# Windowed attention and two feed-forwards: the plan takes VectorE's and GpSimd's SBUF-only instructions to exclude each other, and its order is searched anew

## The chip, the core and the metric

One core of a Trainium2 chip runs one program. Its engines work side by side, each through its own queue in order: TensorE (PE; PEld is its loading of weights), VectorE (DVE), ScalarE (ACT), GpSimd (POOL) and SyncE (SP), which issues most transfers. The metric is the device time of one execution in microseconds (us), as the median of several.

## What is computed

The reference, cut to what matters. The attention keeps four sink columns and a window of 128 keys; its output, 1536 rows of 512, goes through two feed-forwards with 2048 hidden columns.

```python
# batch 2, heads 8, seq 768, head_dim 64; n_sink 4, window 128
scores = scale * np.matmul(q, k.transpose(0, 1, 3, 2))
keep = is_sink | in_window                 # 0 <= row - column < window
scores = np.where(keep, scores, -1e9)
a = softmax(scores)
x = matmul(a, v)                           # as 1536 x 512
h = x @ w_in                               # first feed-forward, 2048 hidden
g = np.where(h >= 1, h, np.where(h <= -1, 0.0, (h + 1) ** 2 / 4))
x = g @ w_out
h = x @ w2_in                              # second feed-forward
r = np.maximum(h, 0.0)
return (r * r) @ w2_out
```

## The kernel before

The attention runs in 24 units (batch, block of 256 rows, pair of heads). In a unit, TensorE turns keys and queries (kind tp), VectorE copies them (tpc), TensorE makes scores for two halves (s), VectorE adds the mask and finds the row's minimum (m), ScalarE takes the exponential (e), VectorE the reciprocal of the sum (n), GpSimd scales the probabilities (pm) and copies the sink columns (sp), TensorE turns the probabilities (x, ts), ScalarE copies them (xc, tsc), TensorE multiplies with the values (av), and ScalarE and VectorE split the result into a high and a low part (xh, xl).

The feed-forwards are split into chunks of 128 hidden columns, 16 for each, in nine passes (PASSES): 3, 3, 4, 3 and 3 chunks for the first, four times 4 for the second. A step is one pass over a range of rows: first the hidden matmuls (L353), for which ScalarE (u; L360 or L362), VectorE (t, L367, which reads only SBUF, then g, L385; in the second feed-forward sq5, L369) and ScalarE and GpSimd (gc, L374, and gl, L378: the high and the low part of the result) work in turn; then the output matmuls (L421), whose sums VectorE adds up in SBUF (ad; L458, L460). The last pass of the first feed-forward also splits the sum for the second (yc, L437, and yl, L439). The twelve steps of passes 0 and 1 (STEPS) have 256 rows and lie between the attention's units; all later ones have 512.

The weights come as 64-bit numbers and are split into two parts by the kernel, each chunk in two halves (w_in, w_out), 64 halves in all: ScalarE takes two pieces of the raw words (ca, L275 and L279), VectorE works on them in four steps (c1 to c4; L292, L293, L285, L295), ScalarE makes the high part (cc, L296) and GpSimd the low one (cl, L297). All halves share one temporary buffer (wt=1), and nine chunks fit into the ring of split weights (six until the attention ends).

The order of all engines is made before the program is written, by a planner in Python. Each step is a Task with an engine, a time for which it holds the engine and one until its result is there (COST: engine, step, took, extra), the tasks it waits for and the buffers it takes. Planner.run always takes the task that can start first; among equals the one with the least key goes first. KEYS, STEPS, SPREAD, LOADS, PARTS and LEAD set the keys; LEAD says by how much the loads and the splits of a late pass's weights rank ahead of the pass itself, whose three steps have keys three apart. The program then issues every engine's instructions in the planned order, and semaphores carry the dependencies. In gaps of TensorE in the attention, warm_gaps puts filler matmuls (L855).

In the planner before, a VectorE task with a last figure over 0 in COST (c1, c2: 0.58; c3: 0.15; c4: 0.2; t: 0.4; t5: 0.3) is lengthened by that share of its overlap with GpSimd tasks. GpSimd tasks are never lengthened:

```python
if t.engine == "DVE" and t.extra:
    more = sum(max(0.0, min(b, at + took) - max(a, at)) for a, b in gps[-3:]) * t.extra
    step, took = step + more, took + more
```

Of the kernel before, what the change touches and what calls it, by code (L numbers as in the profile page):

```python
# [43 lines left out]
    q=2, v=VB, k=KB, p=PB, pt=PTB, sm=4, sp=2, st=2, vs=1, av=2, sc=SCB, tp=TPB, tx=TXB, f=PSF,  # L44
# [1 line left out]
)  # L46
LATE = dict(f=8 - PSF, w=RING - EARLY, G=G1, U=2, T=2)
KEYS = dict(
    q=-56.88, v=92.12, kd=-49.39, kp=-74.72, tp=29.38, tpc=-1.63, kp0=-102.23, s0=0.45,
    m0=-45.61, e0=40.66, s1=0.52, m1=-63.12, e1=101.70, n=2.30, pm0=81.97, sp0=34.55,  # L50
    pm1=-18.03, sp1=39.22, x0=-80.79, xc0=-63.27, x1=8.31, xc1=-25.32, ts=-67.22, tsc=91.12,
    tsl=-29.67, av=38.69, xh=78.19, xl=-127.41,
)
STEPS = [
    (0, 0, 112.72), (0, 256, -26.70), (0, 512, -74.02), (1, 0, -2.04), (1, 256, -58.87),
    (1, 512, 70.12), (0, 1024, -23.65), (0, 768, 33.74), (1, 1024, -32.96), (1, 768, 82.54),
    (0, 1280, -2.66), (1, 1280, 10.87),
]
SPREAD = 8.10, 8.20
LOADS = [24.08, -24.48, 25.55, -33.69, -88.64, 43.67]  # L60
PARTS = [13.07, 11.19, -49.96, 70.04, -43.43, 138.90]
START = 8700.0
LEAD = 125.99, 87.06
LAG = dict(PE=53, ACT=33, DVE=33, POOL=78, SP=40)
COST = dict(
    q=("SP", 2200, 0, 2320), v=("SP", 1100, 0, 1160), kd=("SP", 500, 0, 230), wi=("SP", 500, 0, 1470),
    wo=("SP", 500, 0, 1270), vs=("SP", 900, 0, 200), od=("SP", 500, 0, 800),
    kp=("POOL", 139, 189, 0), kp0=("POOL", 139, 189, 0), vsm=("POOL", 200, 240, 0),
    pm=("POOL", 1012, 1060, 0), pms=("POOL", 562, 615, 0), sp=("POOL", 139, 203, 0),
    cl=("POOL", 1235, 1275, 0), gl=("POOL", 690, 740, 0), gl5=("POOL", 1240, 1290, 0),  # L70
    yl=("POOL", 690, 740, 0), yl5=("POOL", 1240, 1290, 0),
    tp=("PE", 436, 600, 0), s=("PE", 640, 709, 0), ss=("PE", 415, 492, 0), x=("PE", 436, 600, 0),
    xx=("PE", 327, 490, 0), ts=("PE", 218, 380, 0), av=("PE", 1230, 1390, 0), avv=("PE", 790, 870, 0),
    mm=("PE", 120, 283, 0), mm5=("PE", 226.7, 390, 0),
    e=("ACT", 994, 1100, 0), es=("ACT", 780, 880, 0), xc=("ACT", 492, 587, 0), xxc=("ACT", 375, 478, 0),
    tsc=("ACT", 270, 367, 0), xh=("ACT", 270, 370, 0), ca=("ACT", 575, 672, 0), cc=("ACT", 525, 620, 0),
    u=("ACT", 365, 465, 0), gc=("ACT", 310, 405, 0), u5=("ACT", 585, 680, 0), r5=("ACT", 500, 590, 0),
    gc5=("ACT", 525, 620, 0), yc=("ACT", 310, 405, 0), yc5=("ACT", 525, 620, 0), oda=("ACT", 450, 2500, 0),
    tpc=("DVE", 600, 686, 0), m=("DVE", 700, 780, 0), ms=("DVE", 430, 505, 0), n=("DVE", 375, 375, 0),
    tsl=("DVE", 335, 417, 0), xl=("DVE", 335, 417, 0), c1=("DVE", 425, 425, 0.58),  # L80
    c2=("DVE", 425, 425, 0.58), c3=("DVE", 687, 687, 0.15), c4=("DVE", 685, 685, 0.2),
    t=("DVE", 335, 418, 0.4), g=("DVE", 335, 420, 0), ad=("DVE", 335, 417, 0),
    t5=("DVE", 600, 690, 0.3), g5=("DVE", 600, 690, 0), ad5=("DVE", 600, 687, 0),
    sq5=("DVE", 600, 690, 0), mask=("DVE", 1156, 1156, 0), vsc=("DVE", 1600, 1600, 0),
)
TURNS = "tp", "x", "xx", "ts"
CUTS = ((0, 3, 6, 10, 13, 16), (0, 4, 8, 12, 16))
PASSES = [
# [30 lines left out]
class Planner:  # L119
# [28 lines left out]
    def switch(self, last, t):  # L148
        if last is None or t.engine != "PE":
            return 0.0  # L150
        if t.kind in ("s", "ss"):
            return 90.0
        if last.kind in TURNS:
            return 50.0 if t.kind in TURNS else -80.0
        return 0.0

    def run(self):
        free = {pool: [(0.0, i) for i in range(n)] for pool, n in self.slots.items()}
        ready = {e: [] for e in LAG}
        idle = {e: self.begin for e in LAG}  # L160
        dma, gps, pe = self.begin, [(0.0, 0.0)], None
        for t in self.tasks:
            t.wait, t.ready = len(t.after), self.begin
            if not t.wait:
                ready[t.engine].append(t)
        order = []
        while len(order) < len(self.tasks):
            best = None
            for e, tasks in ready.items():
                for t in tasks:  # L170
                    at = self.starts(t, free)
                    if at is not None:
                        c = (max(at, idle[e] + self.switch(pe, t)), t.key, t)
                        if best is None or c[:2] < best[:2]:
                            best = c
            assert best, [(e, [t.kind for t in tasks]) for e, tasks in ready.items()]
            at, _, t = best
            ready[t.engine].remove(t)
            step, took = t.step, t.took
            if t.engine == "DVE" and t.extra:  # L180
                more = sum(max(0.0, min(b, at + took) - max(a, at)) for a, b in gps[-3:]) * t.extra
                step, took = step + more, took + more
            t.start = at
            idle[t.engine] = at + step
            if t.engine == "PE":
                pe = t
            if t.engine == "SP":
                dma = max(at + step + 900, dma) + t.extra
                t.end = dma + 1100
            else:  # L190
                t.end = at + took
            if t.engine == "POOL":
                gps.append((at, t.end))
            for h in t.takes:
                first = min(free[h.pool])
                free[h.pool].remove(first)
                h.slot = first[1]
            for h in t.uses:
                h.left -= 1
                h.end = max(h.end, t.end)  # L200
                if not h.left:
                    free[h.pool].append((h.end, h.slot))
            order.append(t)
            for x, begun in t.next:
                x.wait -= 1
                same = x.engine == t.engine and t.engine != "SP"
                lag = (0 if t.engine == "PE" else 34) if same else LAG[x.engine]
                end = t.start + t.step if same and t.engine == "PE" else t.end
                x.ready = max(x.ready, t.start if begun else end + lag)
                if not x.wait:  # L210
                    ready[x.engine].append(x)
        return order
# [697 lines left out]
def plan_ffn(line, ffn, weights, stage, wtmp, units):  # L910
# [5 lines left out]
    for n, key in enumerate([key for chunks in PASSES for key in chunks]):  # L916
        ps = [key in chunks for chunks in PASSES].index(True)
        raw, ring = [Hold("wr"), Hold("wr")], Hold("w")
        rings[key] = ring
        load = LOADS[n] if n < EARLY else first[ps] - LEAD[0] + 0.1 * PASSES[ps].index(key)  # L920
        part = PARTS[n] if n < EARLY else first[ps] - LEAD[1] + 0.1 * PASSES[ps].index(key)
        step = 0.3 if n < EARLY else 0.05
# [19 lines left out]
    for ps, off, at in steps:  # L942
# [8 lines left out]
        n = len(st["chunks"])  # L951
        spread = SPREAD if early else (0.02, 0.02)
        mid = SPREAD[0] * n if early else 0.5
        for i, key in enumerate(st["chunks"]):
# [330 lines left out]
```

## Time and profile before

| what | us |
|---|---|
| median of three runs | 671.12 |
| the runs | 670.5 to 671.51 |
| the profiled execution | 670.44 |
| its span, first to last instruction | 668.6 |

The profile is one execution, taken by the hardware. Its times count from the first instruction, and busy time is that of instructions that work, not of those that wait. Matmuls overlap each other, so TensorE's busy time runs ahead of its real pace. A wait is put down to what released it last. The page gives PE 96%, DVE 64%, ACT 49% and POOL 45% of the span as busy.

### The profile page before, as it was taken

How to read it: one execution, taken by the hardware profiler on the slowest of the kernel's cores; microseconds unless marked ns; L12 is line 12 of the kernel's file. 1: busy time of each engine (PE TensorE's matmuls, PEld its weight loads, DVE VectorE, ACT ScalarE, POOL GpSimd, SP SyncE). 2: the span in 40 equal slices, each digit the busy share in tenths (PEclk: the TensorE clock that was granted, in tenths of full speed). 3: DMA queues.
4: the chain of work that ended last, by engine and by line, in shares of the span. 5: the costliest groups of instructions: out<-in, count | busy, mean ns of one | idle time of the engine just before them, and what ended most of it. 6: DMA issues, size and time to landing. Idle time of an engine off the chain costs nothing.

```text
span 668.6 us, 9983 instructions
## 1 busy us (share of the span) xinstructions
PE 644.4 (96%) x3572; PEld 528.7 (79%) x3572; DVE 431.2 (64%) x911; ACT 329.4 (49%) x718; POOL 301.9 (45%) x310
## 2 busy tenths in 40 slices
PE   8989899999999999999999998999999999999997
PEld 6666677878999977877878776888888888888886
DVE  5897987875576777769797887654655366222222
ACT  3797877764545545444545555443553255112210
POOL 2565744742533454444445777343444254213311
PEclk9999999999999999999999999999999999999999
DMA  5863731210021222212212112220222020000011
GB/s 123 220 175 81 198 100 59 77 48 1 1 65 63 67 92 64 94 64 71 88 63 95 63 33 81 83 90 31 68 91 95 1 94 32 0 1 31 33 64 69
DMA packets 64187, 47.94 MB, mean 72 GB/s; under 512 B 39936, under 2 KB 58624, under 8 KB 64128
## 3 DMA queue, kind: packets, MB, share of 16 engines
q1 hardware_dynamic: 63296, 46.69, 23.4%
q8 instruction: 30, 0.49, 0.3%
q10 hardware_dynamic: 832, 0.52, 0.2%
q14 instruction: 29, 0.24, 0.1%
HBM read 43.01 MB, written 3.15 MB: 69 GB/s over the span
## 4 chain that ended last, share of the span: by engine, by line
PE 43%; DVE 7%; ACT 2%; POOL 2%; issue 1%; DVEq 0%; POOLq 0%
PE o L421 23%; PE h L353 20%; DVE wx L285 2%; DVE t L367 2%; POOL g L378 1%; DVE wx L293 1%; DVE u L385 1%; DVE wx L292 1%; DVE wx L295 1%; POOL w L297 1%; ACT u L360 1%; ACT wx L275 1%; ACT g L374 0%; ACT w L296 0%; DVE acc L460 0%
## 5 line engine op out<-in xcount | busy, mean ns | idle before, releaser
L353 PE MATMUL h<-x,w 128*128 128x512 f32 (+1 forms) x1368 | 275.6, 357 | 1.5 <-DVE u L385 1.3
L353 PEld LDWEIGHTS h<-x,w 128*128 128x128 f32 x1368 | 228.6, 189 | 42.2 <-DVE u L385 2.5
L297 POOL TENSOR_TENSOR w<-wx,w 128x512 fp32r<-128x512 f32 x64 | 83.3, 1301 | 147.9 <-ACT w L296 142.6
L421 PE MATMUL o<-g,w 128*128 128x256 f32 (+1 forms) x792 | 145.5, 336 | 4.0 <-POOL g L378 3.7
L421 PEld LDWEIGHTS o<-g,w 128*128 128x128 f32 x792 | 120.2, 189 | 26.0 <-POOL g L378 8.8
L421 PE MATMUL o<-w,g 128*128 128x512 f32 (+1 forms) x588 | 133.7, 386 | 2.1 <-POOL g L378 2.1
L421 PEld LDWEIGHTS o<-w,g 128*128 128x128 f32 x588 | 108.5, 188 | 25.6 <-POOL g L378 3.4
L378 POOL TENSOR_TENSOR g<-t,g 128x512 fp32r<-128x512 f32 x48 | 65.7, 1369 | 94.1 <-ACT g L374 82.0
L378 POOL TENSOR_TENSOR g<-u,g 128x256 fp32r<-128x256 f32 (+1 forms) x66 | 72.5, 1102 | 62.0 <-ACT g L374 39.2
L460 DVE TENSOR_TENSOR acc<-o,acc 128x512 f32<-128x512 f32 (+1 forms) x109 | 59.4, 564 | 58.7 <-PE o L421 58.5
L296 ACT CAST w<-wx 128x512 fp32r<-128x512 f32 x64 | 39.7, 621 | 97.3 <-DVE wx L295 97.0
L369 DVE SCALAR_TENSOR_TENSOR t<-h,u 128x512 f32<-128x512 f32 x48 | 33.1, 690 | 66.3 <-ACT u L362 38.4
L367 DVE SCALAR_TENSOR_TENSOR t<-u 128x256 f32<-128x256 f32 (+1 forms) x66 | 46.2, 701 | 31.3 <-ACT u L360 31.3
L687 POOL TENSOR_TENSOR p<-p,sm 128x520 f32<-128x520 f32 (+1 forms) x48 | 49.3, 1040 | 32.7 <-DVE sm L680 19.7
L362 ACT ACTIVATE u<-h 128x512 f32<-128x512 f32 x48 | 28.6, 597 | 67.8 <-PE h L353 67.1
L275 ACT ACTIVATE wx<-wraw 128x512 f32<-128x512 f32 x64 | 42.8, 668 | 35.4 <-POOL w L297 35.0
L285 DVE SCALAR_TENSOR_TENSOR wx<-wraw,wx 128x512 int32<-128x512 int32 x64 | 57.3, 895 | 1.3
L672 ACT ACTIVATE p<-p,sm 128x260 f32<-128x260 f32 (+1 forms) x96 | 46.6, 489 | 16.5 <-DVE sm L663 16.5
L295 DVE CUSTOM_DVE_ANT_0 wx<-wx,wy 128x1024 uint16<-128x1024 uint16 x64 | 50.7, 792 | 2.8
L292 DVE TENSOR_SCALAR wx<-wx 128x512 f32<-128x512 f32 x64 | 35.8, 560 | 23.6 <-ACT wx L275 23.4
L360 ACT ACTIVATE u<-h,half 128x256 f32<-128x256 f32 (+1 forms) x66 | 37.5, 569 | 24.0 <-PE h L353 18.1
L374 ACT CAST g<-t 128x512 fp32r<-128x512 f32 x48 | 29.7, 619 | 29.2 <-DVE t L369 29.1
(73 smaller groups left out, 562.8 us busy)
## 6 DMA issues: line engine op xcount, KB each, us to landing
wraw<-in_moe_w_in_dram SPq DMA_DIRECT2D x32, 512.0 KB, 3.7
wraw<-in_moe_w_out_dram SPq DMA_DIRECT2D x32, 512.0 KB, 3.2
vr<-in_v_dram SPq DMA_DIRECT2D x24, 128.0 KB, 3.1
qr<-in_q_dram SPq DMA_DIRECT2D x22, 128.0 KB, 2.4
kr<-in_k_dram SPq DMA_DIRECT2D x22, 128.0 KB, 2.7
out_dram<-acc SPq DMA_DIRECT2D x10, 256.0 KB, 2.0
k<-k SPq DMA_DIRECT2D x16, 64.0 KB, 2.2
qr<-in_q_dram SPq DMA_DIRECT2D x4, 64.0 KB
```

Of the source, the lines that this page charges most:

```text
L275: nc.scalar.activation(s["x"], f32(s["r"][:, :, 1]), AF.Abs, scale=65536.0)
L285: nc.vector.scalar_tensor_tensor(s["xi"], s["r"][:, :, 1], -(1 << 31), s["xi"], ALU.bitwise_and, ALU.bitwise_or)
L295: ("c4", lambda: nc.vector.tensor_tensor(s["xi"], s["xi"], s["yi"], ALU.add)),
L297: ("cl", lambda: nc.gpsimd.tensor_tensor(s["w"][:, 1], s["x"], f32(s["w"][:, 0]), ALU.subtract)),
L353: nc.tensor.matmul(s["h"], w[:, a, c * P : (c + 1) * P], x[:, b, c, sl], start=n == 0, stop=n == 11)
L360: nc.scalar.activation(s["u"], s["h"], AF.Relu, bias=self.half, scale=0.5)
L367: nc.vector.scalar_tensor_tensor(t, s["u"], 1.0, s["u"], ALU.min, ALU.mult)
L378: nc.gpsimd.tensor_tensor(g[:, 1], s["u" if ffn == 0 else "t"], f32(g[:, 0]), ALU.subtract)
L421: nc.tensor.matmul(s["o"], lhs, rhs, start=n + i + j == 0, stop=n == len(chunks) - 1 and i == 1)
L460: self.nc.vector.tensor_tensor(dst, o, dst, ALU.add)
L672: self.nc.scalar.activation(s[:, e], s[:, e], AF.Exp, bias=sm[:, 0, u, e : e + 1], scale=-1.0, accum_out=sm[:, 1, u, e : e + 1],)
L687: self.nc.gpsimd.tensor_tensor(s, s, r, ALU.mult)
```

## The change

The planner now gives the four split steps, t, t5, the reciprocal (n), the mask and the sink's split (vsc) a flag in place of a share. A flagged VectorE task and any GpSimd task exclude each other: the later one waits until FRONT (137 ns) ahead of the other's end, and is lengthened by that wait, whichever engine it is on. Several durations in COST are changed. KEYS, STEPS, SPREAD, LOADS, PARTS and LEAD have new values, and with them the order of all engines. The instructions themselves are the same, save for the filler matmuls, whose number follows from the plan.

```diff
--- before.py
+++ after.py
@@ -46,43 +46,44 @@
 )
 LATE = dict(f=8 - PSF, w=RING - EARLY, G=G1, U=2, T=2)
 KEYS = dict(
-    q=-56.88, v=92.12, kd=-49.39, kp=-74.72, tp=29.38, tpc=-1.63, kp0=-102.23, s0=0.45,
-    m0=-45.61, e0=40.66, s1=0.52, m1=-63.12, e1=101.70, n=2.30, pm0=81.97, sp0=34.55,
-    pm1=-18.03, sp1=39.22, x0=-80.79, xc0=-63.27, x1=8.31, xc1=-25.32, ts=-67.22, tsc=91.12,
-    tsl=-29.67, av=38.69, xh=78.19, xl=-127.41,
+    q=-77.73, v=115.34, kd=-78.11, kp=-59.27, tp=17.96, tpc=13.94, kp0=-85.43, s0=0.28,
+    m0=-74.97, e0=13.09, s1=1.05, m1=-127.76, e1=174.18, n=8.73, pm0=175.82, sp0=17.36,
+    pm1=-85.55, sp1=68.18, x0=-123.31, xc0=-34.66, x1=9.42, xc1=-66.70, ts=-16.95, tsc=105.60,
+    tsl=-38.41, av=204.26, xh=5.18, xl=-205.56,
 )
 STEPS = [
-    (0, 0, 112.72), (0, 256, -26.70), (0, 512, -74.02), (1, 0, -2.04), (1, 256, -58.87),
-    (1, 512, 70.12), (0, 1024, -23.65), (0, 768, 33.74), (1, 1024, -32.96), (1, 768, 82.54),
-    (0, 1280, -2.66), (1, 1280, 10.87),
+    (0, 0, 63.97), (0, 256, 32.53), (0, 512, -50.01), (1, 512, 7.34), (1, 0, 12.28),
+    (1, 256, 83.53), (0, 1024, -27.14), (1, 1024, 44.68), (0, 768, -51.16), (1, 768, 149.57),
+    (0, 1280, -5.46), (1, 1280, 21.91),
 ]
-SPREAD = 8.10, 8.20
-LOADS = [24.08, -24.48, 25.55, -33.69, -88.64, 43.67]
-PARTS = [13.07, 11.19, -49.96, 70.04, -43.43, 138.90]
+SPREAD = 18.66, 7.44
+LOADS = [18.58, -47.20, 114.98, 3.08, 7.62, -108.53]
+PARTS = [26.07, -15.08, -13.13, 80.77, -203.16, 128.40]
 START = 8700.0
-LEAD = 125.99, 87.06
+LEAD = 173.43, 3.08
 LAG = dict(PE=53, ACT=33, DVE=33, POOL=78, SP=40)
 COST = dict(
     q=("SP", 2200, 0, 2320), v=("SP", 1100, 0, 1160), kd=("SP", 500, 0, 230), wi=("SP", 500, 0, 1470),
     wo=("SP", 500, 0, 1270), vs=("SP", 900, 0, 200), od=("SP", 500, 0, 800),
-    kp=("POOL", 139, 189, 0), kp0=("POOL", 139, 189, 0), vsm=("POOL", 200, 240, 0),
+    kp=("POOL", 139, 189, 0), kp0=("POOL", 139, 189, 0), vsm=("POOL", 470, 515, 0),
     pm=("POOL", 1012, 1060, 0), pms=("POOL", 562, 615, 0), sp=("POOL", 139, 203, 0),
     cl=("POOL", 1235, 1275, 0), gl=("POOL", 690, 740, 0), gl5=("POOL", 1240, 1290, 0),
     yl=("POOL", 690, 740, 0), yl5=("POOL", 1240, 1290, 0),
-    tp=("PE", 436, 600, 0), s=("PE", 640, 709, 0), ss=("PE", 415, 492, 0), x=("PE", 436, 600, 0),
-    xx=("PE", 327, 490, 0), ts=("PE", 218, 380, 0), av=("PE", 1230, 1390, 0), avv=("PE", 790, 870, 0),
+    tp=("PE", 436, 620, 0), s=("PE", 640, 709, 0), ss=("PE", 415, 492, 0), x=("PE", 436, 633, 0),
+    xx=("PE", 327, 490, 0), ts=("PE", 218, 400, 0), av=("PE", 1230, 1390, 0), avv=("PE", 790, 870, 0),
     mm=("PE", 120, 283, 0), mm5=("PE", 226.7, 390, 0),
-    e=("ACT", 994, 1100, 0), es=("ACT", 780, 880, 0), xc=("ACT", 492, 587, 0), xxc=("ACT", 375, 478, 0),
+    e=("ACT", 1000, 1010, 0), es=("ACT", 784, 792, 0), xc=("ACT", 492, 587, 0), xxc=("ACT", 375, 478, 0),
     tsc=("ACT", 270, 367, 0), xh=("ACT", 270, 370, 0), ca=("ACT", 575, 672, 0), cc=("ACT", 525, 620, 0),
     u=("ACT", 365, 465, 0), gc=("ACT", 310, 405, 0), u5=("ACT", 585, 680, 0), r5=("ACT", 500, 590, 0),
     gc5=("ACT", 525, 620, 0), yc=("ACT", 310, 405, 0), yc5=("ACT", 525, 620, 0), oda=("ACT", 450, 2500, 0),
-    tpc=("DVE", 600, 686, 0), m=("DVE", 700, 780, 0), ms=("DVE", 430, 505, 0), n=("DVE", 375, 375, 0),
-    tsl=("DVE", 335, 417, 0), xl=("DVE", 335, 417, 0), c1=("DVE", 425, 425, 0.58),
-    c2=("DVE", 425, 425, 0.58), c3=("DVE", 687, 687, 0.15), c4=("DVE", 685, 685, 0.2),
-    t=("DVE", 335, 418, 0.4), g=("DVE", 335, 420, 0), ad=("DVE", 335, 417, 0),
-    t5=("DVE", 600, 690, 0.3), g5=("DVE", 600, 690, 0), ad5=("DVE", 600, 687, 0),
-    sq5=("DVE", 600, 690, 0), mask=("DVE", 1156, 1156, 0), vsc=("DVE", 1600, 1600, 0),
+    tpc=("DVE", 600, 686, 0), m=("DVE", 700, 780, 0), ms=("DVE", 430, 505, 0), n=("DVE", 375, 375, 1),
+    tsl=("DVE", 335, 417, 0), xl=("DVE", 335, 417, 0), c1=("DVE", 425, 425, 1),
+    c2=("DVE", 425, 425, 1), c3=("DVE", 687, 687, 1), c4=("DVE", 685, 685, 1),
+    t=("DVE", 335, 418, 1), g=("DVE", 335, 420, 0), ad=("DVE", 335, 417, 0),
+    t5=("DVE", 600, 690, 1), g5=("DVE", 600, 690, 0), ad5=("DVE", 600, 687, 0),
+    sq5=("DVE", 600, 690, 0), mask=("DVE", 1156, 1156, 1), vsc=("DVE", 1900, 1900, 1),
 )
+FRONT = 137
 TURNS = "tp", "x", "xx", "ts"
 CUTS = ((0, 3, 6, 10, 13, 16), (0, 4, 8, 12, 16))
 PASSES = [
@@ -158,7 +159,7 @@
         free = {pool: [(0.0, i) for i in range(n)] for pool, n in self.slots.items()}
         ready = {e: [] for e in LAG}
         idle = {e: self.begin for e in LAG}
-        dma, gps, pe = self.begin, [(0.0, 0.0)], None
+        dma, pe, port = self.begin, None, dict(DVE=0.0, POOL=0.0)
         for t in self.tasks:
             t.wait, t.ready = len(t.after), self.begin
             if not t.wait:
@@ -177,9 +178,11 @@
             at, _, t = best
             ready[t.engine].remove(t)
             step, took = t.step, t.took
-            if t.engine == "DVE" and t.extra:
-                more = sum(max(0.0, min(b, at + took) - max(a, at)) for a, b in gps[-3:]) * t.extra
-                step, took = step + more, took + more
+            if t.engine == "POOL" or t.engine == "DVE" and t.extra:
+                other = port["DVE" if t.engine == "POOL" else "POOL"]
+                wait = max(0.0, other - at - FRONT)
+                step, took = step + wait, took + wait
+                port[t.engine] = at + took
             t.start = at
             idle[t.engine] = at + step
             if t.engine == "PE":
@@ -189,8 +192,6 @@
                 t.end = dma + 1100
             else:
                 t.end = at + took
-            if t.engine == "POOL":
-                gps.append((at, t.end))
             for h in t.takes:
                 first = min(free[h.pool])
                 free[h.pool].remove(first)
```

## Rows read from the trace of the kernel before

**Rows 1.** Stretches: us; PE, PEld, DVE, ACT, POOL busy (instructions); clock; DMA share; GB/s.

```profile
20.00:140.00 120.00, 111.46 (x877) 83.74 (x874) 102.48 (x323) 93.76 (x277) 71.47 (x102) 1.00 0.47 122
140.00:240.00 100.00, 99.10 (x763) 91.19 (x763) 68.47 (x162) 51.37 (x118) 42.63 (x51) 1.00 0.13 43
240.00:360.00 120.00, 117.58 (x513) 94.91 (x512) 92.36 (x145) 56.46 (x93) 51.62 (x38) 1.00 0.24 76
360.00:417.50 57.50, 53.41 (x227) 41.58 (x225) 45.67 (x60) 32.12 (x58) 42.91 (x34) 1.00 0.20 64
417.50:664.00 246.50, 246.22 (x1096) 204.11 (x1096) 110.08 (x173) 87.90 (x148) 86.50 (x66) 1.00 0.16 53
360.00:420.00 60.00, 55.72 (x237) 43.50 (x236) 47.44 (x63) 33.21 (x60) 44.29 (x35) 1.00 0.21 68
180.00:200.00 20.00, 19.95 (x169) 19.30 (x168) 12.64 (x29) 9.45 (x20) 6.13 (x7) 1.00 0.16 51
```

**Rows 2.** The chain that ended last, one of its 21 even blocks: start, us, what.

```profile
424.34 10.88 PE h L353 x48
```

**Rows 3.** Waits, 20 to 140 us, then 360 to 417.5: total, times, longest us.

```profile
PEld s L651 <- DVE sm L663: 6.1, 10, 1.6
PEld tx L703 <- POOL p L687: 4.2, 8, 1.0
...
PEld o L421 <- POOL g L378: 6.6, 7, 1.7
```

**Rows 4.** VectorE lines, whole span: ns min/median/max, first and last start.

```profile
L292 DVE TENSOR_SCALAR wx<-wx x64: 396/426/1067, 22.2 to 564.5; 128x512 f32<-128x512 f32 x64
L293 DVE TENSOR_SCALAR wx<-wx x64: 409/427/1528, 22.7 to 564.9; 128x512 int32<-128x512 int32 x64
L285 DVE SCALAR_TENSOR_TENSOR wx<-wraw,wx x64: 660/693/1799, 27.5 to 565.4; 128x512 int32<-128x512 int32 x64
L295 DVE CUSTOM_DVE_ANT_0 wx<-wx,wy x64: 660/692/1780, 29.3 to 567.2; 128x1024 uint16<-128x1024 uint16 x64
L369 DVE SCALAR_TENSOR_TENSOR t<-h,u x48: 677/692/692, 396.6 to 653.7; 128x512 f32<-128x512 f32 x48
```

**Rows 5.** Instructions in order of time: start us, us, what.

```profile
397.18 1.30 POOL L378 TENSOR_TENSOR g<-u,g 128x512 fp32r<-128x512 f32 x1 [1.22 <-ACT g L374]
397.23 1.53 DVE L293 TENSOR_SCALAR wx<-wx 128x512 int32<-128x512 int32 x1
```

**Rows 6.** VectorE groups, 360 to 420 us: busy us, mean ns, idle before.

```profile
L285 DVE SCALAR_TENSOR_TENSOR wx<-wraw,wx 128x512 int32<-128x512 int32 x7 | 8.2, 1165 | 0.1
L293 DVE TENSOR_SCALAR wx<-wx 128x512 int32<-128x512 int32 x7 | 7.2, 1028 | 0.2
L292 DVE TENSOR_SCALAR wx<-wx 128x512 f32<-128x512 f32 x8 | 6.1, 763 | 5.1 <-ACT wx L275 5.1
L367 DVE SCALAR_TENSOR_TENSOR t<-u 128x512 f32<-128x512 f32 x6 | 6.1, 1013 | 3.2 <-ACT u L360 3.2
L295 DVE CUSTOM_DVE_ANT_0 wx<-wx,wy 128x1024 uint16<-128x1024 uint16 x7 | 5.7, 808 | 0.2
```

**Rows 7.** The same groups of VectorE, 20 to 140 us.

```profile
L295 DVE CUSTOM_DVE_ANT_0 wx<-wx,wy 128x1024 uint16<-128x1024 uint16 x11 | 9.6, 876 | 0.1
L285 DVE SCALAR_TENSOR_TENSOR wx<-wraw,wx 128x512 int32<-128x512 int32 x11 | 9.1, 826 | 0.2
...
L293 DVE TENSOR_SCALAR wx<-wx 128x512 int32<-128x512 int32 x11 | 6.4, 582 | 0.2
```

**Rows 8.** Stretches for one line each, L297, then L362: us, busy (instructions), as rows 1.

```profile
0.00:443.50 443.50, 62.65 (x48) 1.00 0.29 84
...
0.00:470.60 470.60, 7.16 (x12) 1.00 0.28 81
```

**Rows 9.** Groups of the whole span, as rows 6.

```profile
L297 POOL TENSOR_TENSOR w<-wx,w 128x512 fp32r<-128x512 f32 x64 | 83.3, 1301 | 147.9 <-ACT w L296 142.6 <-PE h L353 5.1
...
L275 ACT ACTIVATE wx<-wraw 128x512 f32<-128x512 f32 x64 | 42.8, 668 | 35.4 <-POOL w L297 35.0
```

## The prediction

> **What bounds the kernel now.** I read the shares of the page first, then the span cut into stages, then the chain that ended last, then the durations of the instructions that the plan's new rule names. TensorE is busy for 111.5 of 120, 99.1 of 100, 117.6 of 120 us and so on, and its granted clock is 1.00 in every stage [rows 1], the 2.4 GHz level. But its busy time says little, because matmuls overlap. The pace says more. From 417.5 us on, the chain is even blocks of 48 matmuls in 10.88 us, 226.7 ns each, of which one row stands for 21 [rows 2]; 1096 matmuls take 246.5 us there [rows 1]. No order of the other engines can shorten that stretch.
>
> Ahead of it the pace is lower, and the stages differ. Between 240 and 360 us there are 513 matmuls: 513 x 0.2267 = 116.3 us of work in 120, a loss of 3.7 us. Between 360 and 417.5 us, 227 x 0.2267 = 51.5 us of work in 57.5, a loss of 6.0 us [rows 1, 2]. Between 20 and 140 us the matmuls have many shapes, so I take the weight loads as the measure: at full pace they fill 19.30 us of 20 (180 to 200 us), 96.5%, and here 83.74 us of 120 [rows 1]. 83.74 / 0.965 = 86.8 us of work, so about 33 us of slack (an estimate). Between 140 and 240 us the same sum gives 91.19 / 0.965 = 94.5 us of 100, 5.5 us. Some 48 us lie idle behind the first 20 us; the question is how much of it comes from what the change is about.
>
> The waits say who is late. In 20 to 140 us TensorE's weight loads wait for VectorE's row minimum (6.1 us) and GpSimd's scaled probabilities (4.2 us); in 360 to 417.5 us for GpSimd's g alone (6.6 us) [rows 3]. VectorE is busy for 102.5 of 120 us in the first of these stages [rows 1]: it has little left.
>
> **Whether the new rule is true.** VectorE's steps of the weight split that read only SBUF (L292, L293, L285, L295) and the square (L367) have uneven durations: L285 has a median of 693 ns and a maximum of 1799, L293 427 and 1528. L369, which reads the product from PSUM, runs between 677 and 692 in all 48 cases [rows 4]. At 397.23 us an L293 lasts 1.53 us: it began 0.05 us behind a GpSimd subtraction that ended at 398.48, and ended 0.28 us behind that [rows 5]. So the later one waits for the earlier one nearly to its end, and about 0.427 - 0.28 = 0.15 us of its time lies inside the other's. The changed plan says just this (exclusion, with a front of 137 ns), and marks just the instructions that are uneven here. The plan before charged VectorE 15 to 58% of the overlap and GpSimd nothing. What I expect from better foresight is a better order, not less work: both plans issue the same work, save for filler matmuls.
>
> The page "SBUF — State Buffer", section "Who interferes with whom", of the Trainium skill says that VectorE and GpSimd share one pair of ports by an exclusive lock, and that the order of issue decides who blocks. The durations above agree. It speaks against a large gain too: by it order can't remove the exclusion, only choose who waits; what that would make of the time is the second rival below.
>
> **What the changed plan does, part by part.**
>
> *The delays themselves.* In 360 to 420 us the five groups [rows 6], against their medians [rows 4] (L367 against L369, of the same size), were held for 7 x (1165 - 693) = 3.3, 7 x (1028 - 427) = 4.2, 8 x (763 - 426) = 2.7, 7 x (808 - 692) = 0.8 and 6 x (1013 - 692) = 1.9 us, in all 12.9 us of VectorE's 47.4 us. In 20 to 140 us L295, L285 and L293 were held for 11 x (876 - 692) + 11 x (826 - 693) + 11 x (582 - 427) = 2.0 + 1.5 + 1.7 = 5.2 us [rows 4, 7], and GpSimd's instructions by an amount that no one row gives.
>
> *20 to 140 us.* Here VectorE is the dense engine and the waits end on it or on GpSimd behind it. If all 5.2 us went, and VectorE bound throughout, the stage would be 5.2 us shorter; should the new order of the attention's steps be worse than the old, I set the other end at the same 5.2 us. I take 2 us, some third, because only some of TensorE's waits name these two engines: 6.1 + 4.2 us [rows 3] against 33 us of slack. Range -5 to +5.
>
> *140 to 240 us.* 5.5 us of slack in a hundred; VectorE at 68%. I take 0, the cover being its idle third [rows 1]; -2 to +3.
>
> *240 to 417.5 us.* The port is the bound near the end. In 360 to 420 us the VectorE groups need 7 x 0.693 + 7 x 0.427 + 8 x 0.426 + 7 x 0.692 + 6 x 0.692 = 20.2 us without delay, and GpSimd was busy for 44.3 us [rows 1, 4, 6]: 64.5 us for a port that two engines share, in 60 us. Two things fall together there, the splitting of the first feed-forward's result for the second and the split of later weights. The weights come early: the 48th half of 64 (the last of pass 6's chunks) is split by 443.5 us, while until 470.6 us only the 12 hidden tiles of pass 5 have begun their way through ScalarE [rows 8]. That is 27 us of air. The change lowers LEAD's second term from 87.06 to 3.08: the key of a pass's split falls from far above all matmul steps to about that of the pass before. With exclusion in the plan, moving splits behind 417.5 us, where GpSimd is busy for 86.5 of 246.5 us [rows 1], costs TensorE nothing as long as the 27 us hold. So I take 3.5 of the last stage's 6.0 us and 1 of the 3.7 before it: 4.5 us. Ends: 9.7 us if all the loss goes, -8 if the splits come too late (first rival).
>
> *Loads, lead-in, tail.* LEAD's first term goes from 125.99 to 173.43: loads of late weights rank earlier on SyncE's queue, where nothing else is left but key copies and outputs; nothing, and it can't make the end earlier. The first 20 us and the stores at the end hold the same steps as before; 0, -1 to +2. The other new figures of the table (transposes, exponentials, the sink's clear and split) change no instruction, only where the planner believes it to stand. The new table counts the reciprocal and the mask as holding the port; these are small, and a false hold can only place other work a little differently.
>
> *Sum.* 2 + 0 + 4.5 + 0 = 6.5 us. The profiled execution took 670.44 us (span 668.6 and 1.8 around it); 670.44 - 6.5 = 663.9. The median of the runs stands 0.68 us above that execution, so 664.6 us.
>
> **The rivals.**
>
> *Splits too late: slower.* A split half is one chain on one temporary buffer: with undisturbed durations three ScalarE steps at L275's 0.668, 0.426 + 0.427 + 0.693 + 0.692 on VectorE and 1.301 on GpSimd, 5.5 us [rows 4, 9]; with the VectorE durations of 360 to 420 us (0.763 + 1.028 + 1.165 + 0.808 = 3.8) [rows 6] it is 7.1 us. The first pass of the second feed-forward needs 8 halves: 44 or 57 us. The pass before lasts 3 steps of 72 matmuls, 3 x 72 x 0.2267 = 49 us. If the split starts with that pass, as the new key says among equals, it decides at 6.1 us a half: under it nothing is lost, at 7.1 us TensorE stands for 8 us at the border. Then the third term is -8 and the result 670.44 - 2 + 8 + 0.68 = 677. For it: the key. Against it: the plan starts whatever can start first and uses the key only to break ties, so splits also fill idle time of VectorE, which has 177.5 - 92.4 - 45.7 = 39 us of it between 240 and 417.5 us [rows 1].
>
> *Exclusion moved, not lessened: the same.* The sum of work at the port is unchanged, what one instruction no longer waits another does; TensorE's late operands are other ones. 0 to 1.3 us either way, 671.1. For it: 64.5 us wanted in 60. Against it: that is one stage, and the next has room.
>
> *The attention is repacked: much faster.* VectorE idles 17.5 us of 20 to 140 us. If the search, seeing collisions for the first time, closes half of that, 8.8 us, in place of my 2, the sum is 13.3 and the time 657.8; with the whole loss of 240 to 417.5 us as well it is 652.6. For it: 33 us of slack, and all the keys of the attention move. Against it: the chain from score to value is long, and engines wait for each other there rather than for the port.
>
> **How the numbers follow.** Forecast (660 to 669.7) 0.52, much faster (under 660) 0.15, the same 0.13, slower 0.20. A measurement of this kernel can tell about 0.2%, 1.3 us, from no change. Faster is 0.52 + 0.15 = 0.67. For 8 in 10 I leave about 0.08 below and 0.12 above: from 655 us, between the two sums of the last rival, to 675 us, just short of the slower one's 677. The likeliest case is one of gain, and its own range is 660 to 669.7.
>
> **What would show it.** Right: VectorE's L285 and L293 in the stretch that ends the first feed-forward with means near 0.9 and 0.7 us in place of 1165 and 1028 ns; fewer than 6.6 us of waits for g there; the steady pace of 48 in 10.88 us beginning some 6 us earlier; more split halves behind that point. Wrong: L421 or L353 waiting for GpSimd's w (L297) at a pass border shows the first rival; unchanged means with the waits elsewhere show the second; a first stage shorter by over 6 us shows the third. I am wrong altogether if the chip's order drifts from the plan so far that a collision planned away comes back at another place.

## The result and the profile after

The changed kernel takes 656.06 us in the median (655.26 to 656.36) against 670.9 us for the kernel before (four executions of each): a ratio of 0.978, 95% interval 0.976 to 0.979. That is 14.8 us less, where 6.5 had been forecast. The direction is right and the time lies inside the wide range (655 to 675 us), but the gain is more than double the forecast: the time is below the likeliest case's own range (660 to 669.7 us), where the prediction gave the rival "much faster" a chance of 0.15. The profiled execution took 656.22 us, with a span of 654.4 where the kernel before had 668.6.

First the stages of the changed kernel, with the columns of [rows 1]; the stage from 417.5 us ends at 650 us because this kernel ends earlier.

```profile
20.00:140.00 120.00, 114.13 (x894) 86.16 (x893) 107.66 (x331) 95.27 (x286) 74.86 (x107) 0.99 0.47 123
140.00:240.00 100.00, 99.59 (x769) 93.68 (x768) 71.15 (x159) 51.33 (x114) 41.50 (x46) 1.00 0.16 49
240.00:360.00 120.00, 120.00 (x531) 99.27 (x530) 90.46 (x142) 55.83 (x92) 52.43 (x39) 1.00 0.22 71
360.00:417.50 57.50, 57.50 (x256) 47.62 (x255) 42.20 (x59) 30.81 (x55) 39.45 (x32) 1.00 0.18 56
417.50:650.00 232.50, 232.18 (x1036) 192.66 (x1034) 121.28 (x173) 90.06 (x149) 84.93 (x65) 1.00 0.18 59
360.00:420.00 60.00, 60.00 (x267) 49.70 (x266) 44.66 (x61) 31.77 (x57) 40.88 (x33) 1.00 0.18 55
```

There are 531 matmuls in 240 to 360 us where there were 513, and 256 in 360 to 417.5 us where there were 227 [rows 1]. At 0.2267 us each [rows 2] that is 4.1 + 6.6 = 10.7 us: the whole loss of these stages is gone, and TensorE runs at its pace from there to the end. By the weight loads, 20 to 140 us holds (86.16 - 83.74) / 0.965 = 2.5 us more work and 140 to 240 us (93.68 - 91.19) / 0.965 = 2.6 us more. These two are too large together: the spans differ by 668.6 - 654.4 = 14.2 us, which leaves 14.2 - 10.7 = 3.5 us for everything outside 240 to 417.5 us. (The mix of shapes differs, and four more filler matmuls are counted.) The chain that ended last, by engine, of the kernel before and then of the changed one:

```profile
PE 43%; DVE 7%; ACT 2%; POOL 2%; issue 1%; DVEq 0%; POOLq 0%
```

```profile
PE 91%; DVE 4%; ACT 3%; issue 1%; POOL 1%; DVEq 0%; ACTq 0%; POOLq 0%
```

The two lines are not to be compared as they stand: the chain of the kernel before could be followed back only to 298 us, 55% of its span, and TensorE has 43 of these 55, the other engines coming in until 417.5 us. From 298 us to the end TensorE has 77% of the chain before and 99% of the changed one's.

What did *not* go away is the collisions. The page's first part, of the kernel before and of the changed one:

```profile
PE 644.4 (96%) x3572; PEld 528.7 (79%) x3572; DVE 431.2 (64%) x911; ACT 329.4 (49%) x718; POOL 301.9 (45%) x310
```

```profile
PE 640.0 (98%) x3576; PEld 532.5 (81%) x3576; DVE 444.1 (68%) x911; ACT 330.9 (51%) x718; POOL 300.3 (46%) x310
```

The same 911 VectorE instructions are busy for 12.9 us longer, so held for longer in all, and GpSimd's for 1.6 us less. But 11.2 of the 12.9 us lie behind 417.5 us (121.28 us in place of 110.08 for 173 instructions each [rows 1]), where TensorE is at its pace in both kernels. In 360 to 420 us the five groups of [rows 6] now read (columns as there; every line number is one higher):

```profile
L286 DVE SCALAR_TENSOR_TENSOR wx<-wraw,wx 128x512 int32<-128x512 int32 x7 | 7.9, 1126 | 0.1
L296 DVE CUSTOM_DVE_ANT_0 wx<-wx,wy 128x1024 uint16<-128x1024 uint16 x7 | 7.5, 1064 | 0.2
L293 DVE TENSOR_SCALAR wx<-wx 128x512 f32<-128x512 f32 x7 | 5.6, 799 | 1.3 <-ACT wx L276 1.3
L368 DVE SCALAR_TENSOR_TENSOR t<-u 128x512 f32<-128x512 f32 x5 | 5.1, 1027 | 2.5 <-ACT u L361 2.5
...
L294 DVE TENSOR_SCALAR wx<-wx 128x512 int32<-128x512 int32 x7 | 4.6, 652 | 0.1
```

L286 is held nearly as long as before (a mean of 1126 ns in place of 1165), L296 longer, L294 less. And yet TensorE hardly waits for any of it. Its waits in this kernel, for 180 to 420 us and then for 20 to 140 us (total, times, longest us):

```profile
PEld o L422 <- POOL g L379: 0.2, 1, 0.2
...
PEld s L652 <- DVE sm L664: 6.7, 12, 2.0
...
PEld tx L704 <- POOL p L688: 1.0, 2, 0.5
```

The wait for g, 6.6 us before in 360 to 417.5 us alone [rows 3], is 0.2 us in 180 to 420, where the kernel before had 12.2:

```profile
PEld o L421 <- POOL g L378: 12.2, 19, 1.7
```

In the attention the wait for GpSimd's probabilities fell from 4.2 to 1.0 us, that for VectorE's minimum stayed.

Where the delays went: the 48th split half, of which [rows 8] showed 27 us of air, now starts its last instruction at 455.75 us, while the 13th hidden tile of the second feed-forward starts on ScalarE at 456.45. These are the two, of the changed kernel, in order of time:

```profile
455.75 1.29 POOL L298 TENSOR_TENSOR w<-wx,w 128x512 fp32r<-128x512 f32 x1 [5.57 <-ACT w L297]
456.45 0.60 ACT L363 ACTIVATE u<-h 128x512 f32<-128x512 f32 x1 [0.78 <-PE h L354]
```

The air has been used up. Little of it is split work that left the crowded stage: by 417.5 us 42 halves are split where the kernel before had 43. The splits keep about their old times there and come 13 us later behind it, while the steps come 14 us earlier. So the splits take the delays, and the steps' own chain is spared most of them.

### The profile page after: what moved, and what is told of

The parts are those of the page before. It is cut to its first block, busy times and chain, and to the rows that moved or that the text cites. A ratio compares the mean times of both kernels' runs of the same rounds, so it can differ in the third digit from the quotient of the medians.

```text
span 654.4 us, 9990 instructions
## 1 busy us (share of the span) xinstructions
PE 640.0 (98%) x3576; PEld 532.5 (81%) x3576; DVE 444.1 (68%) x911; ACT 330.9 (51%) x718; POOL 300.3 (46%) x310
## 4 chain that ended last, share of the span: by engine, by line
PE 91%; DVE 4%; ACT 3%; issue 1%; POOL 1%; DVEq 0%; ACTq 0%; POOLq 0%
PE o L422 40%; PE h L354 40%; PE s L652 3%; PE av L745 3%; PE tx L704 2%; PE tp L627 1%; DVE p L664 1%; ACT pt L711 1%; ACT p L673 1%; PE warm_a L856 1%; DVE k L640 1%; PE warm_c L856 1%; DVE wx L296 0%; DVE x L755 0%; PE ts L717 0%
## 5 line engine op out<-in xcount | busy, mean ns | idle before, releaser
L422 PE MATMUL o<-g,w 128*128 128x256 f32 (+1 forms) x792 | 142.6, 334 | 0.4 <-DVE u L386 0.4
L379 POOL TENSOR_TENSOR g<-t,g 128x512 fp32r<-128x512 f32 x48 | 63.9, 1334 | 75.7 <-ACT g L375 52.5
L297 ACT CAST w<-wx 128x512 fp32r<-128x512 f32 x64 | 39.7, 621 | 87.9 <-DVE wx L296 87.8
L296 DVE CUSTOM_DVE_ANT_0 wx<-wx,wy 128x1024 uint16<-128x1024 uint16 x64 | 55.4, 866 | 1.5
L286 DVE SCALAR_TENSOR_TENSOR wx<-wraw,wx 128x512 int32<-128x512 int32 x64 | 52.0, 813 | 1.2
L293 DVE TENSOR_SCALAR wx<-wx 128x512 f32<-128x512 f32 x64 | 41.1, 642 | 15.8 <-ACT wx L276 15.5
L375 ACT CAST g<-u 128x256 fp32r<-128x256 f32 (+1 forms) x66 | 32.5, 502 | 29.6 <-DVE u L386 22.4
```

The costliest lines, as they stand in the source:

```text
L286: nc.vector.scalar_tensor_tensor(s["xi"], s["r"][:, :, 1], -(1 << 31), s["xi"], ALU.bitwise_and, ALU.bitwise_or)
L293: ("c1", lambda: nc.vector.tensor_scalar(s["x"], s["x"], 2.0, None, ALU.max)),
L296: ("c4", lambda: nc.vector.tensor_tensor(s["xi"], s["xi"], s["yi"], ALU.add)),
L379: nc.gpsimd.tensor_tensor(g[:, 1], s["u" if ffn == 0 else "t"], f32(g[:, 0]), ALU.subtract)
L422: nc.tensor.matmul(s["o"], lhs, rhs, start=n + i + j == 0, stop=n == len(chunks) - 1 and i == 1)
```

## The experiments

Three theories were put against each other first. One: the later rank of the splits (LEAD), which the prediction had named. Two: the rule of exclusion in the plan. Three: the new keys of the attention.

**LEAD alone, both ways.** The kernel before with the new LEAD, and the changed kernel with the old:

```diff
-LEAD = 125.99, 87.06
+LEAD = 173.43, 3.08
```

> The kernel before with one thing of the change: LEAD = 173.43, 3.08, so that a late pass's split of weights ranks just ahead of the pass before instead of far ahead of everything. Theory 1 (the prediction's step: the splits stood in front of the steps' own chain, and the later rank takes them away): most of the 9.7 us that TensorE lost between 240 and 417.5 us comes back, 661 to 666 us, and the waits of the output matmuls for g in 360 to 417.5 us fall from 6.6 us to under 2. Theory 2 (the rule of exclusion in the plan does it) and theory 3 (the new keys of the attention do it): within 1.5 us of 671, the loss where it was.

> The changed kernel with LEAD = 125.99, 87.06, as before. Theory 1: TensorE loses 5 to 10 us again between 180 and 420 us, 661 to 666 us. Theories 2 and 3: within 1.5 us of 656.

Measured: 671.75 us against 671.24 (ratio 1.0013, 1.0003 to 1.0022), and 656.09 us (0.977, 0.976 to 0.979), as the changed kernel itself. Theory one falls: LEAD brings no gain by itself, and without it none is lost. In the first of the two the stretch from 240 to 360 us still holds 513 matmuls, the number of before:

```profile
240.00:360.00 120.00, 117.92 (x513) 95.48 (x512) 91.78 (x144) 56.46 (x93) 51.56 (x38) 1.00 0.24 75
```

**The rule alone, by place.** The planner of both kernels in one, the rule used for tasks that start behind a time (before's keys and durations), or ahead of one (the changed kernel's). The code is shortened:

```diff
+                if at >= 180e3:        # rule_early: if at < 240e3
                     other = port["DVE" if t.engine == "POOL" else "POOL"]
                     wait = max(0.0, other - at - FRONT)
                     step, took = step + wait, took + wait
+                elif t.engine == "DVE":
+                    more = sum(...) * SHARE[t.kind]     # the old shares
+                    step, took = step + more, took + more
```

> The kernel before with all its keys, its LEAD and its durations; the planner keeps the old shares of overlap for tasks that it starts ahead of 180 us and uses the exclusion for all behind that. So the attention's order is that of before, and the feed-forward's order changes by the rule alone. Theory 2: TensorE's 12 us of loss between 180 and 420 us mostly goes, 659 to 663 us. Theories 1 and 3: no gain from the rule by itself, 669 to 673 us.

> The changed kernel with all its keys; the planner uses the exclusion for tasks that it starts ahead of 240 us and the old shares of overlap behind that. The attention's order is that of the changed kernel. Theory 2: the loss between 240 and 420 us comes back, 5 to 10 us, 661 to 666 us. Theories 1 and 3: within 1.5 us of 656, because the later stage gets its air from LEAD or from the earlier end of the attention.

Measured: 660.08 us (ratio 0.983, 0.982 to 0.985) and 665.5 us (0.9915, 0.990 to 0.993). Theory two stands. The first gains 11.2 us with the attention as before. Here are its stages behind that and its wait for g in 180 to 420 us, then two VectorE groups of 240 to 420 us, of the kernel before and of this run (L285 is now L296, L367 is L378):

```profile
240.00:360.00 120.00, 119.67 (x527) 98.48 (x526) 89.82 (x141) 55.93 (x92) 52.43 (x38) 1.00 0.23 71
360.00:417.50 57.50, 57.50 (x256) 47.60 (x255) 44.79 (x60) 30.91 (x55) 42.34 (x33) 1.00 0.20 65
```

```profile
PEld o L432 <- POOL g L389: 1.4, 3, 0.8
```

```profile
L285 DVE SCALAR_TENSOR_TENSOR wx<-wraw,wx 128x512 int32<-128x512 int32 x25 | 26.7, 1068 | 0.6
L367 DVE SCALAR_TENSOR_TENSOR t<-u 128x512 f32<-128x512 f32 x27 | 23.4, 868 | 15.0 <-ACT u L360 15.0
```

```profile
L378 DVE SCALAR_TENSOR_TENSOR t<-u 128x512 f32<-128x512 f32 x27 | 25.2, 935 | 9.0 <-ACT u L371 8.7
L296 DVE SCALAR_TENSOR_TENSOR wx<-wraw,wx 128x512 int32<-128x512 int32 x23 | 22.0, 955 | 0.4
```

There are 527 and 256 matmuls, full pace from 360 us on, and 1.4 us of waits for g in place of 12.2. Yet the square, a step of TensorE's own supply, is held longer than before (935 against 868 ns); it starts with less idle time ahead of it. The split's L285 is held less (955 against 1068 ns). Against the medians of [rows 4], the four split steps and the square were held for 26.7 us before and are for 24.2 here: 2.5 us less, little beside the 11.2 us gained. In the second, the changed kernel without the rule behind 240 us, the wait for g is back, here for 360 to 417.5 us:

```profile
PEld o L432 <- POOL g L389: 5.1, 5, 1.7
```

**Slower means in place of the rule.** Behind 180 us every affected task gets a fixed excess instead (the edit against the run with the rule behind 180 us):

```diff
-                    wait = max(0.0, other - at - FRONT)
-                    step, took = step + wait, took + wait
+                    step, took = step + FLAT.get(t.kind, 0), took + FLAT.get(t.kind, 0)
```

> The kernel before, keys and plan as before ahead of 180 us; behind that no rule and no shares, but every task of the split, the square and GpSimd's subtractions is lengthened by a fixed sum, its mean excess in the trace of before between 180 and 420 us (c1 175, c2 183, c3 308, c4 108, t 141, t5 183, cl 26, gl 55, gl5 187, yl 118, yl5 204 ns). Theory A (the planner only has to know that these engines are slower on the mean): as good as the rule, 658 to 662 us. Theory B (it has to know which instruction waits for which): clearly behind the rule, 664 to 671 us.

> As the run with flat sums behind 180 us, with half of each sum (c1 88, c2 92, c3 154, c4 54, t 70, t5 92, cl 13, gl 28, gl5 94, yl 59, yl5 102 ns). Theory A (a plan with truer mean durations is enough): 658 to 663 us. Theory B (it has to know which instruction waits for which): 664 to 671 us.

> As the run with flat sums behind 180 us, with the full sums for the steps' own chain (t 141, t5 183, gl 55, gl5 187, yl 118, yl5 204 ns) and none for the split. Theory A: 658 to 663 us, since g is planned to come as late as it does on the mean. Theory B: 664 to 671 us.

Measured: 670.16 us (0.9983, 0.9973 to 0.9993), 666.86 us (0.9936, 0.992 to 0.9953) and 669.04 us (0.9967, 0.9955 to 0.998). The first decides nothing by itself, because it loses at one place what it gains at others: TensorE stands there for a late weight chunk.

```profile
240.01 0.73 PE L363 MATMUL h<-x,w 128*128 128x512 f32 x2 [4.01 <-ACT w L306]
241.93 4.63 PE L363 MATMUL h<-x,w 128*128 128x512 f32 x10 [1.19 <-POOL w L307]
```

Behind that, from 248 to 417.5 us, its waits for g are 3.3 us where the kernel before has 10.8 and the run with the rule none; but a TensorE that stands gives the other engines time, so this can't be put down to the means. The other two have their chunks nearly in time (TensorE waits 1.9 and 0.5 us for split weights in 180 to 420 us, 5.8 us in the first) and get 4.4 and 2.3 us of the rule's 11.2. So truer means are worth something, and the rule more than twice as much as the better of these two. Full sums for all tasks with the chunk in time were not tried, and how near they come to the rule stays open.

**The rule in one direction.** VectorE waits for GpSimd in the plan, GpSimd never waits (the edit against the run with the rule behind 180 us):

```diff
-                    other = port["DVE" if t.engine == "POOL" else "POOL"]
+                    other = 0.0 if t.engine == "POOL" else port["POOL"]
```

> The kernel before, as before ahead of 180 us; behind that the exclusion in one direction: VectorE's marked tasks wait for GpSimd in the plan, GpSimd never waits for VectorE. In the trace of before VectorE's excess between 180 and 420 us is about 32 us and GpSimd's about 9 us. If the larger side is what counts: 659 to 662 us. If TensorE's waits for g come from GpSimd's own delays, which this plan doesn't see: 664 to 670 us.

Measured: 663.17 us (0.9877, 0.9861 to 0.9894), between the two expectations: 8.0 of the 11.2 us.

**Whose order it is.** The plan is made twice: first with the one way of counting, then with the other, while the order of the named engines is held to that of the first plan.

```diff
+                    if e in self.fixed and t.key[1] != self.fixed[e][at_of[e]]:
+                        continue
                     at = self.starts(t, free)
```

> The order of TensorE is that of the plan with exclusion behind 180 us (197 of its 873 tasks stand elsewhere than before); ScalarE, VectorE and GpSimd are then planned around it with the old shares. Theory C (the gain lies in TensorE no longer reaching for g too early): 658 to 663 us. Theory D (it lies in the order of VectorE and GpSimd, which work off what is urgent first): 667 to 672 us.

> The order of TensorE is exactly that of before; ScalarE, VectorE and GpSimd are planned around it with the exclusion behind 180 us. Theory C: TensorE still reaches for g too early, 667 to 672 us. Theory D: 658 to 663 us.

> The orders of ScalarE, VectorE and GpSimd are exactly those of the plan with exclusion behind 180 us; TensorE is planned around them with the old shares (89 of 873 tasks stand elsewhere than in that plan). If the order of these three engines carries the gain: 658 to 663 us. If the gain lies in how the orders fit together, as two runs suggest in which TensorE's order alone was new or alone was old: 664 to 672 us.

Measured: 675.9 us (1.0064, 1.0047 to 1.008), 671.2 us (0.9999, 0.9989 to 1.0009) and 668.63 us (0.9961, 0.9947 to 0.9975). Neither TensorE's order alone nor that of the other three carries the gain; with TensorE's alone the kernel is slower than before, and the other three's bring 2.4 us. The waits of weight loads for g in 180 to 420 us, first with TensorE's order new, then with it old:

```profile
PEld o L436 <- POOL g L393: 11.9, 11, 2.1
```

```profile
PEld o L436 <- POOL g L393: 11.6, 13, 2.1
```

Both are near the 12.2 us that the kernel before shows there; with the other three's order new they are 10.5 us. So none of the three mixtures has the gain; it came only where all orders were from one plan. That this plan's times come truer on the chip than the old one's is the likely reason, but planned and measured times were not laid side by side.

**The search.** Three kernels with before's durations: the rule throughout with keys searched anew, the old plan with keys searched anew, and the rule throughout with the old keys.

```diff
-KEYS, STEPS, SPREAD, LOADS, PARTS, LEAD   (of before)
+KEYS, STEPS, SPREAD, LOADS, PARTS, LEAD   (searched; not in rule_oldkeys)
```

> The kernel before with the exclusion in the plan from the start, its old durations, and keys that were searched anew from those of before (not the keys of the changed kernel). If rule and search together make the gain, whatever the keys: 654 to 661 us. If the gain hangs on the changed kernel's keys or on its new durations: 664 us or more.

> The kernel before with its old planner and its old durations, keys searched anew in the same way and for as long as in the run beside it. If a new search by itself brings the gain: 656 to 666 us. If the old plan has nothing left to find that the chip would keep: 669 to 674 us.

> The kernel before with the exclusion in the plan from the start, old durations and old keys, no search. If the rule by itself makes the order better everywhere: 658 to 661 us, as with the rule behind 180 us, or less. If the attention's keys are fitted to the plan that they were searched with: TensorE loses more than before ahead of 180 us and nothing behind it, 662 to 672 us.

Measured: 656.82 us (0.9786, 0.977 to 0.980), 667.32 us (0.9953, 0.9937 to 0.997) and 665.47 us (0.9916, 0.990 to 0.993). With the rule a second, independent search arrives within 1 us of the changed kernel, so neither its particular keys nor its new durations are needed. A search under the old plan gets 3.8 us. (It is one search of each kind.) The rule with the old keys keeps the later gain but loses in the attention, at 140 to 240 us above all (its stages from 140 us on):

```profile
140.00:240.00 100.00, 96.50 (x764) 89.33 (x762) 68.61 (x159) 49.53 (x116) 40.67 (x50) 1.00 0.14 43
240.00:360.00 120.00, 119.99 (x522) 99.23 (x523) 91.58 (x141) 54.87 (x92) 51.46 (x37) 0.99 0.23 71
360.00:417.50 57.50, 57.13 (x253) 46.95 (x252) 43.06 (x61) 31.59 (x56) 42.60 (x34) 1.00 0.21 65
```

There are 89.33 us of weight loads where the kernel before had 91.19 [rows 1]: the old keys were fitted to the plan that they had been searched with.

No kernel here was faster than the changed one.

## Why the prediction was right and where it was wrong

*Right.* The bound (TensorE, at full pace behind 417.5 us) and the losses by stage: 9.7 us had been counted between 240 and 417.5 us, and 10.7 us came back there. The rule: VectorE's unevenness is exclusion, and a plan that knows it makes a better order with the same work. The prediction read this from one instruction; the trace of the kernel before bears it out in all 80 cases (last section). The first term, 2 us for the attention: by its weight loads 2.5, while the spans leave about 3.5 us for it and for 140 to 240 us together. The tail and the lead-in at nothing.

*The term that was mis-sized* is the third, 4.5 us, which measured 10.7. The step that failed: the port, wanted for 64.5 us in 60, was taken to bound TensorE near 417.5 us, so that only 3.5 of 6.0 us could be had. By the same sum the changed kernel wants the port in 360 to 420 us for 7 x 0.693 + 7 x 0.692 + 7 x 0.426 + 5 x 0.692 + 7 x 0.427 = 19.1 us of VectorE and 40.9 of GpSimd, 60.0 us in 60, and TensorE is busy for all of them. The run with the rule behind 180 us has GpSimd busy for 42.3 of the last 57.5 us, hardly less than before's 42.9, and TensorE complete. (GpSimd's busy time also holds its own waits for VectorE, so the sum asks for too much.) A full port bounds only what TensorE needs soon; the prediction had itself found 27 us of air in the splits and then did not let them pay the whole bill. Nor did the splits have to leave the stage: 42 halves are done by 417.5 us in place of 43, so the gain there lies in the order inside it. Of the smaller loss in 240 to 360 us it took 1 of 3.7 us with no reason given, and all came back.

*The cause named for it was wrong.* LEAD was said to move the splits back. By itself it brings nothing, either way (671.75 and 656.09 us). The argument against the first rival, that keys only break ties, was the right one and should have been turned on this step too: behind 417.5 us the splits come later because the exclusion lengthens what the plan counts, not because their key fell. By 443.5 us 48 halves were split before; it is 47 with the new LEAD alone, 45 with the rule alone behind 180 us, and 46 in the changed kernel with either LEAD.

*The sign to look for was wrong too.* L285 and L293 were to fall to means near 0.9 and 0.7 us in 360 to 420 us. L293's fell (652 ns), L285's stayed at 1126, and VectorE's busy time rose by 12.9 us in all. The main gain is not fewer collisions; they moved to where TensorE does not wait.

*140 to 240 us* was set at 0, because VectorE idles for a third of it; by the weight loads 2.6 us came, about as much as in the stage before it.

*The rivals.* Too late splits are real but did not strike here: the run with flat excesses stood for 4.0 and 1.2 us for a late chunk. The second, exclusion only moved, was half right: it moved, and that was the gain. The third came near the time (657.8 us) by luck: it looked for the surplus in the attention, and the surplus was behind it.

What remains beside the rule behind 180 us is about 4.0 us, between 660.08 and 656.06: the attention's new order, with its new durations. (It is 3.6 us by the two gains, 14.8 and 11.2, each against its own measurement of the kernel before.) The new search with the old durations comes to 656.82, so the order carries most of it; the new durations were not tried alone.

The page "SBUF — State Buffer" of the Trainium skill, section "Who interferes with whom", says that the order of issue decides who blocks. The traces agree: the shift of [rows 5], which began second, lasted 1.53 us in place of its median of 0.427. The rival that leaned on it underrated what that choice is worth: 11.2 us in these runs.

## What to carry to other kernels

When an order is made by a plan, put into the plan what one instruction does to another on the other engine: here that was worth 11.2 us, while truer mean durations got 4.4 us at best in three tries and a new search without it 3.8. Judge a change of order by the stage's loss and by how much air the work has that can be put off, not by whether the shared resource is full or whether collisions become fewer. And don't mend one engine's order alone: here it had to come from the same plan as the others'.

## What the runs showed of the hardware

In the trace of the kernel before VectorE and GpSimd took turns without exception. There 80 of the split's four VectorE steps and the squares began while a GpSimd subtraction or scaling still had over 0.2 us to run. Each of them ended so late that only 129 to 145 ns of its undisturbed time (the median of its kind with GpSimd idle) lay inside the other's, whereas all 23 steps for g (L385, which reads the product from PSUM) that began so ended ahead of it. It holds the other way round too: 11 of GpSimd's scalings of 520 columns, 1053 ns undisturbed, began behind such a VectorE instruction and overlapped it by 140 to 144 ns. The plan's FRONT of 137 ns is this overlap. In the changed kernel 94 VectorE instructions began so and 93 of them waited, 21 behind 417.5 us, where it had been 8.

In the changed kernel the granted clock fell to 1.2 GHz (0.50) for 3.4 us from 85.1 us on, while TensorE was busy; ahead of it lay a stretch of waits, with 2.19 us of matmuls in 4 us. The rows are 80 to 84, 86 to 87 and 89 to 90 us, columns as in [rows 1].

```profile
80.00:84.00 4.00, 2.19 (x22) 1.43 (x18) 3.94 (x9) 1.91 (x7) 1.75 (x2) 1.00 0.74 194
...
86.00:87.00 1.00, 1.00 (x7) 1.00 (x6) 0.97 (x3) 1.00 (x5) 0.86 (x2) 0.50 0.65 149
...
89.00:90.00 1.00, 1.00 (x10) 0.87 (x10) 0.78 (x2) 0.00 (x1) 0.67 (x2) 1.00 0.07 14
```

The one execution of that kernel at a mean clock of 1.000 took 655.26 us, the others, at 0.995 to 0.997, 655.9 to 656.36. Of the 19 executions of the kernel before that were measured beside the run with flat excesses, the ten at a mean clock of 0.998 or more took 670.51 to 671.16 us, the nine at 0.995 or 0.996 671.18 to 671.74. In the run with flat excesses it fell likewise behind the 4 us for which TensorE stood (0.50 in 242 to 244 us), and ten matmuls there took 4.63 us, 463 ns each in place of 226.7. A long wait of TensorE can cost more than its length, then, and keeping it supplied can pay a little twice.
